# Second FFN of a decay-attention kernel: inner products by pairs of weight tiles and pairs of token blocks, in 11 products in place of 12

## The chip, the cores and the metric

The kernel runs on one core of a Trainium2 chip. Its five engines are TensorE (PE, matrix products), VectorE (DVE), ScalarE (ACT), GpSimd (POOL) and SyncE (SP, which here issues nearly all DMAs). The metric is the device time of one execution in microseconds (us).

## The reference

A linear attention with decay over 4 x 768 tokens of 8 heads x 48, then two FFNs. Only the last one is changed:

```python
def _moe2_ref(x, w_in, w_out):           # x 3072 x 384, w_in 384 x 2048, w_out 2048 x 384
    h = x @ w_in
    sp = np.where(h > 20.0, h, np.log1p(np.exp(np.minimum(h, 20.0))))
    g = h * np.tanh(sp)                  # Mish
    return (g @ w_out).astype(np.float32)
```

## The kernel before

The 3072 tokens are six blocks j of 512 (`NB`), the model width of 384 is three chunks c of 128 (`KC`), and the 2048 hidden columns are 16 tiles f of 128 (`NF2`). Every operand of a large product is held as two fp32r halves, hi (rounded) and lo (the rest), and `product` makes one 128x128x512 product in three matmuls: weight hi by data hi, weight hi by data lo, weight lo by data hi (lines 253 to 255).

The order of the instructions on each engine is the order of the code (`manual_schedule`); buffers are taken from pools, and an instruction waits where its buffer or its data is not free yet. The parts in the order of time are the attention with the first FFN's first units woven in, the first FFN (units of 27 matmuls: `gate`, `val` and `out` of nine each), and the second FFN. While the last 12 units of the first FFN run (block 5), the 32 split weight tiles of the second FFN are read from DRAM (`w2s`) into the pool `wpool`, 36 slots of 384 KB, as the first FFN's weights in it come free, and they stay there for all six blocks.

The second FFN goes over `units2`, all f of block 0, then all f of block 1, and so on. `ffn2_in` makes one inner tile: three products (nine matmuls) summed in one PSUM bank, and one ACT instruction that reads the bank and writes Mish of it to SBUF (line 928). `split_of` makes the halves: hi by ACT (line 934), lo by DVE (line 935). `ffn2_out` adds a tile's three output products (nine matmuls) to three PSUM accumulators `acc0` to `acc2`, three units (`LAG`) later. After a block's last tile the accumulators are copied out, `acc1` by DVE (line 953), the others by ACT (line 955), and stored. The data of the next block comes from DRAM (`load_mid`) and is split chunk by chunk (`split_mid`).

Banks: three in the pool `ps_at` (name `at`), two in `ps_mm` (`mm`), three accumulators (`ps_acc`).

Of the kernel before, what the change touches and what calls it, by code (L numbers as in the profile page):

```python
# [82 lines left out]
def tile_decay_attention_then_two_ffns(  # L83
# [254 lines left out]
    for n in range(B, PRELOAD):  # L338
# [406 lines left out]
    def opens(c):  # L745
# [110 lines left out]
    for n in range(2, len(units) - NF1):  # L856
# [11 lines left out]
        turn = iter(ticks)  # L868
# [8 lines left out]

    LAG = 3  # L880
    hpool = ctx.enter_context(tc.tile_pool(name="hpool", bufs=3))
    g2pool = ctx.enter_context(tc.tile_pool(name="g2pool", bufs=LAG + 2))
    mpool = ctx.enter_context(tc.tile_pool(name="mpool", bufs=KC))

    def load_mid(j):
        raw = []
        for c in range(KC):
            raw.append(mpool.tile([P, NB], F32, name="rows"))
            rows = slice(c * NB, (c + 1) * NB)
            nc.sync.dma_start(out=raw[c], in_=mid[j][:, rows])  # L890
            if j == 1:
                nc.gpsimd.dma_start(out=raw[c], in_=begun[:, rows], accum_op=ALU.add)
        xs[j, "m"] = (
            raw,
            *(xpools[j % 2].tile([P, KC, NB], F32R, name=f"x_{k}") for k in ("hi", "lo")),
        )

    def split_mid(j, c):
        raw, hi, lo = xs[j, "m"]
        nc.vector.tensor_copy(hi[:, c, :], raw[c])  # L900
        nc.vector.tensor_tensor(
            out=lo[:, c, :], in0=raw[c], in1=f32(hi[:, c, :]), op=ALU.subtract
        )

    for f in range(NF1):
        unit1(len(units) - NF1 + f)
        if f == 2:
            load_mid(0)
        if f in (5, 6, 7):
            split_mid(0, f - 5)  # L910
        for n in range(3 if f else 0):
            weights.tick()
    ffn1_out(*units[-1])

    units2 = [(j, f) for j in range(NJ) for f in range(NF2)]
    N2 = len(units2)
    hs, g2 = {}, {}

    def ffn2_in(n):
        j, f = units2[n]  # L920
        _, hi, lo = xs[j, "m"]
        pool, name = ((ps_at, "at"), (ps_mm, "mm"))[n % 5 in (1, 3)]
        ps = pool.tile([P, NB], F32, name=name)
        wt = weights.until((2, f, 0))
        for c in range(KC):
            product(ps, wt, cols(c), hi[:, c, :], lo[:, c, :], c == 0, c == KC - 1)
        h = hs[n] = hpool.tile([P, NB], F32, name="h")
        nc.scalar.activation(h, ps, AF.Mish)  # L928

    def split_of(n):  # L930

        h = hs.pop(n)
        hi, lo = g2[n] = [g2pool.tile([P, NB], F32R, name=f"g_{k}") for k in ("hi", "lo")]
        nc.scalar.activation(hi, h, AF.Copy)  # L934
        nc.vector.tensor_tensor(out=lo, in0=h, in1=f32(hi), op=ALU.subtract)  # L935

    def ffn2_out(n, ms=range(KC)):
        j, f = units2[n]
# [8 lines left out]
    def ffn2_store(n):
        j, f = units2[n]
        if f == NF2 - 1:
            for m in range(KC):  # L950
                o = opool.tile([P, NB], F32, name="o")
                if m == 1:
                    nc.vector.tensor_copy(o, accs[m])
                else:
                    nc.scalar.activation(o, accs[m], AF.Copy)
                nc.sync.dma_start(out=out[j, :, m * NB : (m + 1) * NB], in_=o)

    nc.scalar.preload_act_table_set("mish")
    for n in range(N2 + LAG):
        if n < N2:  # L960
            ffn2_in(n)
        if n == N2 + LAG - 1:

            for m in range(KC):
                ffn2_out(N2 - 2, [m])
                ffn2_out(N2 - 1, [m])
        elif LAG <= n < N2 + LAG - 2:
            ffn2_out(n - LAG)
        if n < N2:
            split_of(n)  # L970
        if n >= LAG:
            ffn2_store(n - LAG)
        j, f = units2[min(n, N2 - 1)]
        if n < N2 and j + 1 < NJ:
            if f == 6:
                load_mid(j + 1)
            if f in (9, 10, 11):
                split_mid(j + 1, f - 9)


# [79 lines left out]
```

## Time and profile before

| what | value |
|---|---|
| median of three runs | 943.07 us (942.3 to 943.15) |
| the profiled execution: time, span of its instructions | 943.3 us, 941.6 us |
| TensorE busy, granted clock | 932.3 us (99%), 1.000 of full speed |
| VectorE, ScalarE, GpSimd busy | 422.1, 334.9, 172.8 us |
| DMA | 94.97 MB, mean 101 GB/s |

Busy time of PE is the union of matmuls that overlap: one lasts 0.39 us from its start to its modelled end, while the next starts long before that end. What a matmul takes of PE's time is the distance between two starts, which a timeline shows. The span is 1.7 us shorter than the execution's own time.

### The profile page before, as it was taken

What the parts mean: (1) busy time and instruction counts of PE and PEld (TensorE: products, weight loads), DVE (VectorE), ACT (ScalarE), POOL (GpSimd) and SP (SyncE); (2) the same over time, 40 slices, a digit from 0 to 9 for tenths busy, and PEclk for the clock granted to TensorE, in tenths of its full rate; (3) what the DMA queues carried; (4) which work ended last, traced back from release to release, by engine and by line L of the source; (5) the groups of instructions that cost most, each with busy time, mean ns of one, the idle gap of its engine ahead of it and who ended that gap; (6) DMA issues with size and microseconds to landing.
All of it is one profiled execution on the core that took longest, in us unless ns stands there. A gap on an engine that the chain in (4) does not pass through costs nothing.

```text
span 941.6 us, 14268 instructions
## 1 busy us (share of the span) xinstructions
PE 932.3 (99%) x5769; PEld 762.0 (81%) x5769; DVE 422.1 (45%) x764; ACT 334.9 (36%) x674; POOL 172.8 (18%) x162
## 2 busy tenths in 40 slices
PE   9999999999999999999999999999999999999998
PEld 6888877778888888888888888888888888888886
DVE  8898978445787777532223222223113212222111
ACT  6765443324343433312221243233332333323322
POOL 4100221665554565420000010000000000000000
PEclk9999999999999999999999999999999999999999
DMA  9454631325674865310066640010010100200000
GB/s 320 145 144 135 227 126 34 136 102 198 197 239 136 273 200 184 136 52 1 1 222 197 185 100 1 1 68 1 0 68 1 63 5 1 68 1 1 34 1 33
DMA packets 36353, 94.97 MB, mean 101 GB/s; under 512 B 4288, under 2 KB 4672, under 8 KB 36288
## 3 DMA queue, kind: packets, MB, share of 16 engines
q1 hardware_dynamic: 35856, 93.28, 30.1%
q0 software_dynamic: 432, 0.79, 0.5%
q8 instruction: 45, 0.74, 0.3%
q14 instruction: 20, 0.16, 0.1%
HBM read 71.24 MB, written 22.81 MB: 100 GB/s over the span
## 4 chain that ended last, share of the span: by engine, by line
PE 97%; DVE 2%; ACT 0%; issue 0%; DMA 0%; DVEq 0%
PE mm L253 13%; PE mm L255 13%; PE mm L254 13%; PE acc L253 12%; PE acc L254 12%; PE acc L255 12%; PE at L253 5%; PE at L255 5%; PE at L254 5%; PE at L537 3%; PE at L488 2%; PE mm L488 1%; PE at L514 1%; PE at L570 1%; PE acc L446 0%; PE at L506 0%
## 5 line engine op out<-in xcount | busy, mean ns | idle before, releaser
L253 PE MATMUL mm<-x_hi,w_split 128*128 128x512 f32 x543 | 214.3, 395 | 0.0
L255 PE MATMUL mm<-x_hi,w_split 128*128 128x512 f32 x543 | 211.6, 390 | 1.3 <-DVE w_split L207 1.3
L254 PE MATMUL mm<-x_lo,w_split 128*128 128x512 f32 x543 | 211.8, 390 | 0.1
L935 DVE TENSOR_TENSOR g_lo<-h,g_hi 128x512 fp32r<-128x512 f32 x96 | 66.4, 692 | 300.2 <-ACT g_hi L934 300.2
L253 PE MATMUL acc<-g_hi,w_split 128*128 128x512 f32 x483 | 189.3, 392 | 0.0
L254 PE MATMUL acc<-g_lo,w_split 128*128 128x512 f32 x483 | 188.3, 390 | 0.3 <-DVE g_lo L689 0.3
L255 PE MATMUL acc<-g_hi,w_split 128*128 128x512 f32 x483 | 188.0, 389 | 0.0
L681 DVE TENSOR_TENSOR o<-mm,o 128x512 f32<-128x512 f32 x72 | 49.6, 689 | 160.9 <-PE mm L255 122.0
L255 PEld LDWEIGHTS mm<-x_hi,w_split 128*128 128x128 f32 x543 | 101.9, 188 | 23.3 <-DVE w_split L207 1.7
L253 PEld LDWEIGHTS mm<-x_hi,w_split 128*128 128x128 f32 x543 | 101.9, 188 | 23.1 <-issue 0.6
L254 PEld LDWEIGHTS mm<-x_lo,w_split 128*128 128x128 f32 x543 | 102.0, 188 | 20.9 <-DVE x_lo L616 0.4
L253 PEld LDWEIGHTS acc<-g_hi,w_split 128*128 128x128 f32 x483 | 90.7, 188 | 19.8 <-ACT g_hi L683 0.2
L254 PEld LDWEIGHTS acc<-g_lo,w_split 128*128 128x128 f32 x483 | 90.7, 188 | 19.6 <-DVE g_lo L689 1.1
L255 PEld LDWEIGHTS acc<-g_hi,w_split 128*128 128x128 f32 x483 | 90.7, 188 | 19.0
L683 ACT ACTIVATE g_hi<-o 128x512 fp32r<-128x512 f32 x72 | 45.5, 633 | 130.3 <-DVE o L681 129.9
L928 ACT ACTIVATE h<-at 128x512 f32<-128x512 f32 x58 | 34.7, 598 | 154.6 <-PE at L255 154.5
L677 ACT ACTIVATE o<-mm 128x512 f32<-128x512 f32 x71 | 42.1, 593 | 97.8 <-PE mm L255 83.4
L254 PE MATMUL at<-x_lo,w_split 128*128 128x512 f32 x174 | 67.7, 389 | 0.0
L253 PE MATMUL at<-x_hi,w_split 128*128 128x512 f32 x174 | 67.7, 389 | 0.0
L255 PE MATMUL at<-x_hi,w_split 128*128 128x512 f32 x174 | 67.7, 389 | 0.0
L689 DVE TENSOR_TENSOR g_lo<-o,g_hi 128x512 fp32r<-128x512 f32 x72 | 54.5, 758 | 23.7 <-ACT g_hi L683 23.7
L934 ACT ACTIVATE g_hi<-h 128x512 fp32r<-128x512 f32 x96 | 60.7, 632 | 3.1
(115 smaller groups left out, 945.9 us busy)
## 6 DMA issues: line engine op xcount, KB each, us to landing
w_raw<-w SPq DMA_DIRECT2D x68, 384.0 KB, 3.6
rkv_sb<-rkv_t SPq DMA_DIRECT2D x16, 768.0 KB, 5.1
w2s<-w_raw SPq DMA_DIRECT2D x32, 384.0 KB, 4.0
w_split<-w2s SPq DMA_DIRECT2D x32, 384.0 KB, 3.5
n_sb<-rk_n SPq DMA_DIRECT2D x16, 384.0 KB, 5.8
mid<-o SPq DMA_DIRECT2D x18, 256.0 KB, 2.2
rows<-mid SPq DMA_DIRECT2D x18, 256.0 KB, 3.6
y<-o SPq DMA_DIRECT2D x18, 256.0 KB, 2.1
```

What stands on the lines that cost most here:

```text
L253: nc.tensor.matmul(acc, lhsT=wt[:, 0, sl], rhs=hi, start=start, stop=False)
L254: nc.tensor.matmul(acc, lhsT=wt[:, 0, sl], rhs=lo, start=False, stop=False)
L255: nc.tensor.matmul(acc, lhsT=wt[:, 1, sl], rhs=hi, start=False, stop=stop)
L488: nc.tensor.matmul(ps[g][:, i, :], lhsT=a["k"][q, i, :], rhs=a["r"][q, i, :], start=True, stop=True,)
L537: nc.tensor.matmul(ps[q * QUAD : (q + 1) * QUAD, c, :], lhsT=lhsT, rhs=rhs, start=q not in begun_q, stop=ends[q] == n, skip_group_check=True,)
L677: nc.scalar.activation(sg, ps, AF.Silu)
L681: nc.vector.tensor_tensor(out=sg, in0=ps, in1=sg, op=ALU.mult)
L683: nc.scalar.activation(hi, sg, AF.Copy)
L689: eng.tensor_tensor(out=lo, in0=sg, in1=f32(hi), op=ALU.subtract)
L928: nc.scalar.activation(h, ps, AF.Mish)
L934: nc.scalar.activation(hi, h, AF.Copy)
L935: nc.vector.tensor_tensor(out=lo, in0=h, in1=f32(hi), op=ALU.subtract)
```

## The change

It takes the tiles f = 2q and 2q+1 and the blocks j = 2p and 2p+1 together: a cell (p, q), three passes p of eight cells. With a(f,c) the weight chunks, b(c,i) the data chunks, the first two of the three chunks are a 2x2 by 2x2 product of 128x128 and 128x512 pieces, which is made by seven products (Strassen's algorithm in Winograd's form) with sums of weights s1 to s4 and differences of data t1 to t4; the third chunk is made by four plain products. That is 11 products or 33 matmuls in a cell, where the same four inner tiles took 12 products or 36 matmuls. The seven results (regions 1, 2, 6, 5, 7, 3, 4 in this order, one bank each) are added up in SBUF tiles: one ACT copy out of PSUM, seven DVE adds; then Mish is taken by ACT in place. These tiles come from `wpool`.

- The sums of weights are made once per q while the last 12 units of the first FFN run (`sums_of`, called by `beside2` after a unit's `out`), split, and stored to DRAM (`w2z`, and s4 over one chunk of `w2s`).
- `wpool` now holds results, and the weights are read again wherever they are used: `Stream` issues a 384 KB load eight loads ahead of its use, three for a cell and one for each output tile, 168 in all.
- The output products keep their order (all f of block 0, then block 1, ...), but their places are given by the list `events`: none in the first cell, two in each other cell of pass 0, four in each cell of passes 1 and 2, and 18 after the last cell. The halves of a result are made up to three output tiles ahead (`LEAD`).
- The data of a pass is loaded in the third cell of the pass before, and its differences and halves are made in the last cell of that pass (`NEXT`) and in its own first cell (`THEN`); those of pass 0 beside the first FFN (`BESIDE2`).

```diff
-    LAG = 3
...
+    NQ = NF2 // 2
+    AHEAD_W, LEAD = 8, 3
...
+    def sums_of(q):
...
+        nc.vector.tensor_tensor(out=n[:, :, 0], in0=n[:, :, 0], in1=n[:, :, 1], op=ALU.add)
...
+            (s1, a21, a22, ALU.add), (s2, s1, a11, ALU.subtract),
+            (s3, a11, a21, ALU.subtract), (s4, a12, s2, ALU.subtract),
+        ):
+            nc.vector.tensor_tensor(out=o, in0=a, in1=b, op=op)
+        if q + 1 < NQ:
+            load_pair(q + 1)
+        nc.scalar.activation(t[:, 0], f32(t[:, 1]), AF.Copy)
+        nc.vector.tensor_tensor(out=t[:, 1], in0=f32(t[:, 1]), in1=f32(t[:, 0]), op=ALU.subtract)
...
+        nc.sync.dma_start(out=to, in_=t[:, :, :3])
+        nc.sync.dma_start(out=src[1][:, :, :P], in_=t[:, :, 3])
...
+            places = {(0, 0): (), (0, 1): (5, 4)}.get((p, min(q, 1)), (2, 5, 3, 4))
+            for r in R_ORDER:
+                events.append(("region", p, q, r))
+                if r in places:
+                    events.append(("out", *outs[n]))
...
+    NEXT = {1: "b11", 2: "b21 b31", 5: "t1 t2", 7: "t3", 3: "b32"}
+    THEN = {1: "b22", 2: "t4 d3"}
...
+    PARTS2 = {
+        1: (("x", 0, "b11"),),
+        2: (("x", 1, "b21"), ("x", 2, "b31")),
+        6: (("z", 1, "t2"),),
+        5: (("z", 0, "t1"),),
+        7: (("z", 2, "t3"), ("y", 2, "b32")),
+        3: (("y", 0, "b22"), ("x", 2, "b32")),
+        4: (("y", 1, "t4"), ("y", 2, "d3")),
+    }
...
+    def region(n, p, q, r):
         pool, name = ((ps_at, "at"), (ps_mm, "mm"))[n % 5 in (1, 3)]
...
+        if r == 1:
+            nc.scalar.activation(g_tile(1, 1), ps, AF.Copy)
+        elif r == 2:
+            more(g_tile(0, 0), us[1, 1], ps)
+            mish(p, q, 0, 0)
+        elif r == 6:
+            more(us[1, 1], us[1, 1], ps)
+        elif r == 5:
+            more(g_tile(0, 1), us[1, 1], ps)
+        elif r == 7:
+            more(g_tile(1, 0), us[1, 1], ps)
+            more(us[1, 1], us[1, 0], us[5])
+            mish(p, q, 1, 1)
...
```

On TensorE, at a step from one inner tile to the next, the program before has (the last product of a tile in bank `at`, the first of the next in bank `mm`):

```order
L253 MATMUL at_5536<-x_hi_5093,w_split_5099 128x512
L254 MATMUL at_5536<-x_lo_5094,w_split_5099 128x512
L255 MATMUL at_5536<-x_hi_5093,w_split_5099 128x512
L253 MATMUL mm_5552<-x_hi_5093,w_split_5139 128x512
L254 MATMUL mm_5552<-x_lo_5094,w_split_5139 128x512
L255 MATMUL mm_5552<-x_hi_5093,w_split_5139 128x512
```

and the changed program begins its first cell with regions 1, 2 and 6 (`x_hi_5438` is b31 here; `w_split_5483` holds the chunks of tile 0, `w_split_5487` the sums s1 to s3):

```order
L250 MATMUL at_5609<-b11_hi_4971,w_split_5483 128x512
L251 MATMUL at_5609<-b11_lo_4972,w_split_5483 128x512
L252 MATMUL at_5609<-b11_hi_4971,w_split_5483 128x512
L250 MATMUL mm_5615<-b21_hi_4973,w_split_5483 128x512
L251 MATMUL mm_5615<-b21_lo_4974,w_split_5483 128x512
L252 MATMUL mm_5615<-b21_hi_4973,w_split_5483 128x512
L250 MATMUL mm_5615<-x_hi_5438,w_split_5483 128x512
L251 MATMUL mm_5615<-x_lo_5439,w_split_5483 128x512
L252 MATMUL mm_5615<-x_hi_5438,w_split_5483 128x512
L250 MATMUL at_5625<-t2_hi_4975,w_split_5487 128x512
L251 MATMUL at_5625<-t2_lo_4976,w_split_5487 128x512
L252 MATMUL at_5625<-t2_hi_4975,w_split_5487 128x512
```

A bank took nine matmuls before and takes three or six now; the matmuls themselves have the same shape.

On VectorE, in one unit of the first FFN's last block, the program before has the product of the gate (681), the lo half (689), and in three of the units a split of the next data:

```order
L681 TENSOR_TENSOR o<-mm,o 128x512
L689 TENSOR_TENSOR g_lo<-o,g_hi 128x512
L900 CAST x_hi<-rows 128x512
L901 TENSOR_TENSOR x_lo<-rows,x_hi 128x512
L681 TENSOR_TENSOR o<-mm,o 128x512
```

and the changed program has, in eight of the 12 units, the sums of weights between the lo half and the next unit's product (678 and 686 are 681 and 689 of before):

```order
L678 TENSOR_TENSOR o<-mm,o 128x512
L686 TENSOR_TENSOR g_lo<-o,g_hi 128x512
L899 TENSOR_TENSOR x_hi<-x_hi 128x2x256
L906 TENSOR_TENSOR x_lo<-x_hi 128x128
L906 TENSOR_TENSOR x_lo<-x_lo,x_hi 128x128
L906 TENSOR_TENSOR x_lo<-x_hi 128x128
L906 TENSOR_TENSOR x_lo<-x_hi,x_lo 128x128
L910 TENSOR_TENSOR x_lo<-x_lo 128x512
L678 TENSOR_TENSOR o<-mm,o 128x512
```

Six instructions have come in ahead of the next product; the last one waits for an ACT copy.

On VectorE at the end of a block in the second FFN, the program before has lo halves alone around the copy of `acc1`:

```order
L935 TENSOR_TENSOR g_lo_5944<-h_5932,g_hi_5943 128x512
L935 TENSOR_TENSOR g_lo_5969<-h_5957,g_hi_5968 128x512
L953 COPY o_5975<-acc1_5565 128x512
L935 TENSOR_TENSOR g_lo_6006<-h_5991,g_hi_6005 128x512
L935 TENSOR_TENSOR g_lo_6031<-h_6019,g_hi_6030 128x512
```

and the changed program reaches the first such copy, in the first cell of pass 1, at the end of a run of 30 instructions that begins with region 2's add in the last cell of pass 0 (its first rows and its last; `rows` are raw data, lines 981 the differences and lo halves, 1059 the adds):

```order
L1059 TENSOR_TENSOR w_split_6260<-w_split_6249,at_6253 128x512
L981 TENSOR_TENSOR b11_lo_4972<-rows_5779,b11_hi_4971 128x512
L1059 TENSOR_TENSOR w_split_6249<-w_split_6249,mm_6266 128x512
L981 TENSOR_TENSOR b21_lo_4974<-rows_5781,b21_hi_4973 128x512
...
L981 TENSOR_TENSOR x_lo_5581<-rows_5783,x_hi_5580 128x512
L1059 TENSOR_TENSOR w_split_6362<-w_split_6362,mm_6402 128x512
L981 TENSOR_TENSOR g_lo_6398<-w_split_5613,g_hi_6397 128x512
L1059 TENSOR_TENSOR w_split_6412<-w_split_6362,at_6408 128x512
L1110 COPY o_6428<-acc1_5715 128x512
```

The copy has moved behind the data work of the next pass and the adds of two cells.

## Rows read from the trace of the kernel before

**Rows 1.** The page's first part: busy us (share of the span) and instructions of engines.

```profile
PE 932.3 (99%) x5769; PEld 762.0 (81%) x5769; DVE 422.1 (45%) x764; ACT 334.9 (36%) x674; POOL 172.8 (18%) x162
```

**Rows 2.** The page's second part: granted TensorE clock in 40 slices.

```profile
PEclk9999999999999999999999999999999999999999
```

**Rows 3.** The page's fourth part: the chain that ended last, by engine.

```profile
PE 97%; DVE 2%; ACT 0%; issue 0%; DMA 0%; DVEq 0%
```

**Rows 4.** Timeline of PE in the second FFN: start us, duration us, instruction.

```profile
545.91 0.39 PE L253 MATMUL at<-x_hi,w_split 128*128 128x512 f32 x1
...
561.78 0.39 PE L254 MATMUL at<-x_lo,w_split 128*128 128x512 f32 x1
562.00 0.39 PE L255 MATMUL at<-x_hi,w_split 128*128 128x512 f32 x1
562.23 0.39 PE L253 MATMUL acc<-g_hi,w_split 128*128 128x512 f32 x1
...
937.36 0.39 PE L255 MATMUL acc<-g_hi,w_split 128*128 128x512 f32 x1
```

**Rows 5.** Groups from 546 us on: count, busy us, mean ns, idle before.

```profile
L253 PE MATMUL at<-x_hi,w_split 128*128 128x512 f32 x174 | 67.7, 389 | 0.0
L935 DVE TENSOR_TENSOR g_lo<-h,g_hi 128x512 fp32r<-128x512 f32 x96 | 66.4, 692 | 300.2 <-ACT g_hi L934 300.2
L934 ACT ACTIVATE g_hi<-h 128x512 fp32r<-128x512 f32 x96 | 60.7, 632 | 3.1
L928 ACT ACTIVATE h<-at 128x512 f32<-128x512 f32 x58 | 34.7, 598 | 154.6 <-PE at L255 154.5 <-issue 0.2
```

**Rows 6.** Groups of the whole span: DVE instructions like the new ones.

```profile
L681 DVE TENSOR_TENSOR o<-mm,o 128x512 f32<-128x512 f32 x72 | 49.6, 689 | 160.9 <-PE mm L255 122.0 <-issue 19.0 <-ACT o L677 15.7
L616 DVE TENSOR_TENSOR x_lo<-at,x_hi 128x384 fp32r<-128x384 f32 x24 | 13.2, 550 | 5.4 <-ACT x_hi L606 4.7 <-ACT x_hi L611 0.6
L586 DVE TENSOR_TENSOR state<-at,state 48x192 f32<-48x192 f32 x32 | 11.3, 352 | 2.5 <-ACT state L593 2.2
```

**Rows 7.** Timeline of DVE in the second FFN, at the end of block 0.

```profile
616.76 0.69 DVE L935 TENSOR_TENSOR g_lo<-h,g_hi 128x512 fp32r<-128x512 f32 x1 [3.39 <-ACT g_hi L934]
617.37 0.68 DVE L953 COPY o<-acc 128x512 f32<-128x512 f32 x1
```

**Rows 8.** Timeline of DVE and ACT in one unit of the first FFN's last block.

```profile
480.61 0.69 DVE L681 TENSOR_TENSOR o<-mm,o 128x512 f32<-128x512 f32 x1 [3.42 <-PE mm L255]
481.34 0.63 ACT L683 ACTIVATE g_hi<-o 128x512 fp32r<-128x512 f32 x1 [2.18 <-DVE o L681]
482.00 0.69 DVE L689 TENSOR_TENSOR g_lo<-o,g_hi 128x512 fp32r<-128x512 f32 x1 [0.70 <-ACT g_hi L683]
486.73 0.69 DVE L681 TENSOR_TENSOR o<-mm,o 128x512 f32<-128x512 f32 x1 [4.04 <-DMA w_split<-w2s]
```

**Rows 9.** DMA from 473 to 546 us: totals; KB each and median us to landing.

```profile
DMA packets 5476, 14.22 MB, mean 195 GB/s; under 512 B 608, under 2 KB 608, under 8 KB 5472
...
w_split<-w2s SPq DMA_DIRECT2D x32, 384.0 KB, 3.5
...
rows<-mid SPq DMA_DIRECT2D x3, 256.0 KB, 4.6
```

**Rows 10.** Timeline where the second FFN begins: DVE, ACT and SP's queue.

```profile
543.21 0.69 DVE L689 TENSOR_TENSOR g_lo<-o,g_hi 128x512 fp32r<-128x512 f32 x1 [0.70 <-ACT g_hi L683]
...
546.73 1.28 ACT L958 ACT_TABLE_LOAD   x1
...
547.10 1.43 SPq L890 DMA_DIRECT2D rows<-mid  x3
```

**Rows 11.** Windows: us, busy and instructions by engine, PE clock, DMA share, GB/s.

```profile
473.00:546.00 73.00, 73.00 (x323) 60.16 (x322) 20.87 (x32) 15.85 (x26) 0.00 (x0) 1.00 0.62 195
```

More of the change, by code (lines that the diff above doesn't have):

```diff
@@ L115, in tile_decay_attention_then_two_ffns @@
     begun = dram.tile([P, KC * NB], F32, name="begun")
+    w2z = [dram.tile([P, 2, DM], F32, name=f"w2z{q}") for q in range(NF2 // 2)]
     ctx.enter_context(tc.manual_schedule())
@@ L875, in tile_decay_attention_then_two_ffns @@
     first.close()
-    LAG = 3
[L881 to L903, printed above, removed]
-    for f in range(NF1):
[L906 to L912, printed above, removed]
-    ffn1_out(*units[-1])
@@ L915, in tile_decay_attention_then_two_ffns @@
[L915 to L921, printed above, removed]
-        pool, name = ((ps_at, "at"), (ps_mm, "mm"))[n % 5 in (1, 3)]
[L923 to L928, printed above, removed]
@@ L930, in split_of @@
-    def split_of(n):
[L932 to L938, printed above, removed]
+    NQ = NF2 // 2
+    AHEAD_W, LEAD = 8, 3
+    tpool = ctx.enter_context(tc.tile_pool(name="tpool", bufs=1))
+    g2pool = ctx.enter_context(tc.tile_pool(name="g2pool", bufs=LEAD + 2))
@@ new lines, in tile_decay_attention_then_two_ffns @@
+    R_ORDER = (1, 2, 6, 5, 7, 3, 4)
+    outs = [(j, f) for j in range(NJ) for f in range(NF2)]
+    events, n = [], 0
+    for p in range(NJ // 2):
+        for q in range(NQ):
+            places = {(0, 0): (), (0, 1): (5, 4)}.get((p, min(q, 1)), (2, 5, 3, 4))
[3 more added lines that the diff above has]
+                    events.append(("out", *outs[n]))
+                    n += 1
+    events += [("out", *o) for o in outs[n:]]
@@ new lines, in tile_decay_attention_then_two_ffns, with __init__, add, ahead @@
+    class Stream:
+        def __init__(self):
+            self.jobs, self.at, self.got, self.place = [], 0, {}, {}
+            for e in events:
+                if e[0] == "out":
+                    self.add(e, w2s[2 * e[2] + 1])
+                elif e[3] == 1:
+                    q = e[2]
+                    for i, src in enumerate((w2s[4 * q], w2s[4 * q + 2], w2z[q])):
+                        self.add(("in", e[1], q, i), src)
+        def add(self, key, src):
+            self.place[key] = len(self.jobs)
+            self.jobs.append((key, src))
+        def ahead(self, n):
+            while self.at < min(n, len(self.jobs)):
+                key, src = self.jobs[self.at]
+                self.got[key] = wpool.tile([P, 2, DM], F32R, name="w_split")
+                nc.sync.dma_start(out=f32(self.got[key]), in_=src)
+                self.at += 1
+        def get(self, key):
+            self.ahead(self.place[key] + 1 + AHEAD_W)
+            return self.got[key]
@@ new lines, in tile_decay_attention_then_two_ffns, with load_mid, place_ops @@
+    stream = Stream()
+    raws, ops = {}, {}
+    def load_mid(p):
+        for i in range(2):
+            j = 2 * p + i
+            for c in range(KC):
+                t = raws[c, i] = mpool.tile([P, NB], F32, name="rows")
+                rows = slice(c * NB, (c + 1) * NB)
+                nc.sync.dma_start(out=t, in_=mid[j][:, rows])
+                if j == 1:
+                    nc.gpsimd.dma_start(out=t, in_=begun[:, rows], accum_op=ALU.add)
+    def place_ops(i):
+        if i < 2:
+            pair = [xpools[i].tile([P, KC, NB], F32R, name=f"x_{k}") for k in ("hi", "lo")]
+            for c, name in enumerate((("b31", "t3", "b32"), ("b22", "t4", "d3"))[i]):
+                ops[name] = [t[:, c, :] for t in pair]
+        else:
+            for name in ("b11", "b21", "t2", "t1"):
+                ops[name] = [tpool.tile([P, NB], F32R, name=f"{name}_{k}") for k in ("hi", "lo")]
@@ new lines, in less, with split, flush, split_mid @@
+    def less(o, a, b):
+        nc.vector.tensor_tensor(out=o, in0=a, in1=b, op=ALU.subtract)
+    late = []
+    def split(pair, src):
+        hi, lo = pair
+        nc.scalar.activation(hi, src, AF.Copy)
+        late.append(lambda: less(lo, src, f32(hi)))
+    def flush(n):
+        for f in late[:n]:
+            f()
+        del late[:n]
+    def split_mid(name):
+        if name == "t1":
+            less(raws[0, 0], raws[0, 1], raws[0, 0])
+            raws["t2"] = mpool.tile([P, NB], F32, name="rows")
+            less(raws["t2"], raws[1, 1], raws[0, 0])
+        elif name == "t3":
+            less(raws[0, 1], raws[1, 1], raws[0, 1])
+        elif name == "t4":
+            less(raws[1, 0], raws[1, 0], raws["t2"])
+        elif name == "d3":
+            less(raws[2, 0], raws[2, 0], raws[2, 1])
+        at = {"b11": (0, 0), "b21": (1, 0), "b31": (2, 0), "t1": (0, 0), "t2": "t2", "t3": (0, 1),
+              "b32": (2, 1), "b22": (1, 1), "t4": (1, 0), "d3": (2, 0)}[name]
+        split(ops[name], raws[at])
@@ new lines, in tile_decay_attention_then_two_ffns, with beside2 @@
+    NEXT = {1: "b11", 2: "b21 b31", 5: "t1 t2", 7: "t3", 3: "b32"}
+    THEN = {1: "b22", 2: "t4 d3"}
+    BESIDE2 = {3: "b11", 5: "b21", NQ + 1: "t1 t2", NQ + 2: "b31 t3", NQ + 3: "b32"}
+    def beside2(f):
+        if 0 < f <= NQ:
+            sums_of(f - 1)
+        if f == NQ:
+            place_ops(0)
+        for name in BESIDE2.get(f, "").split():
+            split_mid(name)
+        flush(len(late))
+        if f > NQ:
+            stream.ahead(3 * (f - NQ))
+    place_ops(2)
+    load_pair(0)
@@ new lines, in tile_decay_attention_then_two_ffns @@
+    load_mid(0)
+    for f in range(NF1):
+        turn = iter((nothing, lambda: beside2(f), nothing))
+        unit1(len(units) - NF1 + f, nothing, lambda: next(turn)())
+    place_ops(1)
+    for name in ("b22", "t4", "d3"):
+        split_mid(name)
+    flush(len(late))
+    ffn1_out(*units[-1])
+    gs2, splits, us = {}, {}, {}
+    PARTS2 = {
[7 more added lines that the diff above has]
+    }
@@ new lines, in g_tile, with more, mish @@
+    def g_tile(f, i):
+        t = us[f, i] = f32(wpool.tile([P, 2, DM], F32R, name="w_split"))
+        us[f, i] = t.rearrange("p w n -> p (w n)")[:, :NB]
+        return us[f, i]
+    def more(o, a, b):
+        nc.vector.tensor_tensor(out=o, in0=a, in1=b, op=ALU.add)
+    def mish(p, q, f, i):
+        t = gs2[2 * p + i, 2 * q + f] = us.pop((f, i))
+        nc.scalar.activation(t, t, AF.Mish)
+    def region(n, p, q, r):
+        pool, name = ((ps_at, "at"), (ps_mm, "mm"))[n % 5 in (1, 3)]
+        ps = us[r] = pool.tile([P, NB], F32, name=name)
+        for k, (w, c, name) in enumerate(PARTS2[r]):
+            wt = stream.get(("in", p, q, "xyz".index(w)))
+            product(ps, wt, cols(c), *ops[name], k == 0, k == len(PARTS2[r]) - 1)
+        if r == 1:
[11 more added lines that the diff above has]
+            mish(p, q, 1, 1)
+        elif r == 3:
+            more(us[0, 1], us[0, 1], ps)
+            mish(p, q, 0, 1)
+        elif r == 4:
+            more(us[1, 0], us[1, 0], ps)
+            mish(p, q, 1, 0)
@@ L939, in ffn2_out @@
+    def split_of(n):
+        g = gs2.pop(outs[n])
+        pool = gpool if n % (LEAD + 4) < 2 else g2pool
+        splits[outs[n]] = [pool.tile([P, NB], F32R, name=f"g_{k}") for k in ("hi", "lo")]
+        split(splits[outs[n]], g)
+    def ffn2_out(j, f, ms=range(KC)):
         if f == 0:
@@ L941, in ffn2_out @@
                 accs[m] = ps_acc.tile([P, NB], F32, name=f"acc{m}")
-        hi, lo = g2[n]
-        wt = weights.until((2, f, 1))
+        hi, lo = splits[j, f]
+        wt = stream.get(("out", j, f))
         for m in ms:
             product(accs[m], wt, cols(m), hi, lo, f == 0, f == NF2 - 1)
[L947 to L956, printed above, removed]
@@ L958, in tile_decay_attention_then_two_ffns, with ffn2_store @@
-    nc.scalar.preload_act_table_set("mish")
[L959 to L978, printed above, removed]
+    def ffn2_store(j):
+        for m in range(KC):
+            o = opool.tile([P, NB], F32, name="o")
+            if m == 1:
+                nc.vector.tensor_copy(o, accs[m])
+            else:
+                nc.scalar.activation(o, accs[m], AF.Copy)
+            nc.sync.dma_start(out=out[j, :, m * NB : (m + 1) * NB], in_=o)
@@ new lines, in tile_decay_attention_then_two_ffns @@
+    nc.scalar.preload_act_table_set("mish")
+    n_out = n_split = n_region = 0
+    for e in events:
+        pending = len(late)
+        fresh = set(gs2)
+        more_ops = ""
+        if e[0] == "region":
+            _, p, q, r = e
+            region(n_region, p, q, r)
+            n_region += 1
+            if p + 1 < NJ // 2:
+                if q == 2 and r == 1:
+                    load_mid(p + 1)
+                if q == NQ - 1:
+                    more_ops = NEXT.get(r, "")
+            if p and q == 0:
+                more_ops = THEN.get(r, "")
+        else:
+            n_out += 1
+            _, j, f = e
+            if n_out < len(outs) - 1:
+                ffn2_out(j, f)
+            elif n_out == len(outs):
+                for m in range(KC):
+                    ffn2_out(j, f - 1, [m])
+                    ffn2_out(j, f, [m])
+            if f == NF2 - 1:
+                ffn2_store(j)
+        while n_split < min(n_out + LEAD, len(outs)) and outs[n_split] in fresh:
+            split_of(n_split)
+            n_split += 1
+        for name in more_ops.split():
+            split_mid(name)
+        flush(pending)
```

21 lines of the change are left out of this document (17 added, 4 removed).

## The prediction

> **What bounds the kernel now.** I read the page's busy shares first: PE is busy for 99% of the span, DVE for 45%, ACT for 36% [rows 1]. A busy share can be full of waiting, so next the clock and the chain of waits: the granted clock stands at its full level, 2.4 GHz, in all 40 slices [rows 2], and 97% of the chain that ended last is PE's own work [rows 3]. What a matmul takes is read from the timeline: starts in the second FFN lie 0.22 or 0.23 us apart, at the step from an inner tile in bank `at` to the output product in `acc0` too, where PE has waits for ACT and DVE to pass [rows 4]. The whole stage says it more exactly. It has 6 x 16 x 18 = 1728 matmuls; the first starts at 545.91, the last at 937.36: 391.45 / 1727 = 0.2267 us each. So this stage is a gapless row of equal matmuls, and its time is their number times 0.2267. The other engines are only there to be in time: 96 lo halves of 0.692 us on DVE, 96 hi halves of 0.632 us and as many Mish of 0.598 us on ACT (58 of them in the row shown) [rows 5].
>
> **What is removed.** Each of the 24 cells has 33 matmuls of the first product in place of 36: 72 matmuls of the same shape. 72 x 0.2267 = 16.3 us. The output products stay as many. The matmuls of the first FFN and of the attention are untouched.
>
> At this place the Trainium skill would give another price. Its page "TensorE: Matmul & The Clock Gate", section "Back-to-back issue gap", gives about 131 ns per matmul of 512 columns for a sustained row of weight loads and matmuls, and 216 ns for matmuls alone. By the 131 ns the gain would be an estimated 9.4 us. The trace has the same instruction 1728 times at 226.7 ns, so the measurement decides.
>
> **What is added, and where it hides.** A cell with four output tiles lasts (33 + 36) x 0.2267 = 15.64 us on PE (16.32 before), a cell of pass 0 with two lasts (33 + 18) x 0.2267 = 11.56 us, and the first cell, with none, 7.48 us.
>
> (a) DVE gets seven adds in a cell, 168 in all. The nearest row is the gate's product, which reads one operand from PSUM and one from SBUF: 0.689 us [rows 6]. With four lo halves that is 11 x 0.69 = 7.6 us of 15.64. Independent DVE instructions follow each other faster than they last: the copy of `acc1` starts 0.61 us after the lo half ahead of it, which lasts 0.69 [rows 7]. I step through DVE's queue with 0.61 and take 0.69 for the bound.
>
> (b) ACT: one copy, four Mish, four hi halves, 5 x 0.598 + 4 x 0.632 = 5.5 us of 15.64 [rows 5]. Hidden.
>
> (c) Banks. Regions go round five banks, so region n waits until region n-5 is read. The bank held longest is region 5's, which the second add of region 7 still reads; its next user is region 2 of the next cell. In a full cell that add ends some 10.4 us after the cell's start, the next user starts at 16.3. Hidden by 5.9 us. In the first cell, without output products, it is close: see (g).
>
> (d) The sums of weights in the first FFN's last block. A unit lasts 27 x 0.2267 = 6.12 us; DVE is free from the end of a lo half (482.69) to the next gate product (486.73), 4.04 us [rows 8]. In there come one add of 512 columns (0.69), four of 128 columns, an ACT copy (0.63) that DVE waits for, and a last subtraction (0.69). The four small ones: not below 0.14 us (a quarter of 0.55 for 384 columns), not above 0.352 (48 x 192) [rows 6]; two are links of a chain, and I take 0.27. Sum: 0.61 + 1.05 + 0.1 + 0.63 + 0.1 + 0.69 = 3.2 us, within 4.04. If it overruns, the gate's product comes late, and PE needs the bank that it frees only when the next `val` begins, 8.16 - 4.99 = 3.2 us after that product ends. But each pair of source loads may only be issued when the four small sums of the pair before are done. A load lands 3.5 us after its issue, the worst row in this stretch is 4.6 [rows 9]; SP takes about 0.48 us to issue one (1.43 for three, [rows 10]). Round: 0.61 + 1.05 + 0.1 + 0.48 + 3.5 = 5.7 us, under the unit's 6.12; with 4.6 it is 6.8, seven rounds slip 5 us, cover is 0.8 + 3.2, and PE would lose about 1 us. I take 0, being nearer to the 3.5 of 384 KB loads (these have 256 KB).
>
> (e) The weights are read again: 168 loads of 393 KB, seven in a cell of 15.64 us (176 GB/s), one in 2.04 us after the last cell (193 GB/s). The row to compare is the last block of the first FFN, where such loads ran at a mean of 195 GB/s for 73 us and landed 3.5 us after issue [rows 9], while PE started 323 matmuls in 73.0 us, the same 0.226 us [rows 11]. So this traffic doesn't slow the matmuls. Each load is issued eight loads ahead; following the slots and SP's queue through the built program, the shortest lead behind the first cells is 71 matmuls, 16.1 us, against 3.5 to 4.6. It is at the store of block 4, where SP waits for the accumulators' copies. Hidden.
>
> (f) The next pass's data: in the last cell of a pass DVE gets seven lo halves and three differences more, in the next cell three and two more. In pass 0 that last cell is 11.56 us long, and DVE has 9 + 10 = 19 instructions: 11.6 us at 0.61, 13.1 at 0.69. DVE falls behind, and the first to need it is PE at `acc1` of block 1's first output tile. From region 2's add (which may start 2.24 us after the last cell's start) the copy of `acc1` is the 30th instruction. Step by step with ACT's waits in it, at a pace of 0.61, it ends at 21.9 us; PE wants it at 11.56 + 10.2 + 0.68 = 22.4 us (the next cell's seven regions but the last, two output tiles, three matmuls). At 0.69 each, 2.24 + 29 x 0.69 + 0.69 = 22.9, with a few of ACT's waits on top up to 23.9: PE would stand for 0.5 to 1.5 us. I take 0.4. At the next change of pass the last cell is 4.08 us longer for two DVE instructions more: 0.
>
> (g) Where the second FFN begins, DVE's last lo half ends at 543.90 [rows 10]. Behind it come seven instructions, and on ACT three halves, two copies and the table load of 1.28 us ahead of region 1's copy, which so ends near 549.5. Five adds and one lo half later region 5's bank is free, at 553.4 (0.61) to 553.9 (0.69). PE wants it after 36 matmuls, 545.91 + 8.16 = 554.07. 0, by a thin margin.
>
> **Sum.** From the profiled execution's own 943.3 us: - 16.3 + 0.4 = 927.4. That execution is 0.2 above the median of 943.07, against which the time is **927.2 us**.
>
> **Rivals.** A difference of 0.2%, 1.9 us, is about what a measurement of this kernel can tell from none.
>
> 1. DVE or ACT is late at the places (d), (f), (g), and PE stands there. For it: margins of 0.2 to 0.6 us, made with a pace from one pair of rows. Against: DVE's load is 49% in a full cell, so it catches up in the next. At the bounds, 1 + 1.5 + 0.5, and as much again where one lateness hands on another: 928.5 to 932, say 929.5.
>
> 2. Slower: the repeated loads become the bound. Before, nothing was loaded in this stage but data. The point from which it decides is seven loads in 16.32 us, 169 GB/s: at 160 GB/s a cell lasts 17.2 us, and 16 full cells and 18 last tiles (2.46 against 2.04) make 943.3 + 16 x 0.9 + 18 x 0.42 = 965. For it: 66 MB in place of 12.6. Against: the 195 GB/s held in [rows 9] was set by how fast slots came free, not by the DMAs.
>
> 3. The change does nothing: each satisfied wait costs PE something. In the built programs 197 matmuls of this stage wait before, 354 after. At 0.1 us each, 157 x 0.1 = 15.7 us would eat the gain: 942.7. Against: the starts in [rows 4] don't widen where waits stand.
>
> 4. A removed matmul is worth less than the mean distance, because the weight load, not the streaming, set the pace of the rest. If it paid 0.13 in place of 0.2267, 943.3 - 9.4 = 934. By the skill's 131 ns named above this is what would come; nothing in the rows bears it out, as PE's starts are even.
>
> **How the numbers follow.** My forecast (PE's row stays gapless but for under 1.5 us) 0.76, rival 1 0.15, rival 2 0.05, rival 3 0.02, rival 4 0.02. The likeliest time is 927.2, its own range 926.3 to 928.5. Low end of the range: no stall at all and the runs' own spread of 0.8 us under the median, 926.0. High end: most of rival 1, 931.0. That leaves out the rest of it and rivals 2 to 4. Faster by over 0.2%: 0.76 + 0.15 + 0.02 = 0.93; within: 0.02; slower: 0.05.
>
> **What would show it.** Right: 1656 matmuls in the second FFN at 0.2267 us; PE waits of under 1.5 us in all from the first FFN's last block on; region adds of 0.69 us; loads landing in 3.5 to 5 us with no PE wait for `w_split`. Wrong: the distance of starts over 0.23 in cells; PE idle behind `acc1`'s copy at the changes of pass, or behind the gate's product in the first FFN's last block; PE waiting for DMA in cells, above all in those with four output tiles; a granted clock under 1.0.

## The result and the profile after

The changed kernel takes **929.77 us** (median of four runs, 928.75 to 930.14) against 942.92 for the kernel before on the same chip (four runs, 942.3 to 943.15): a ratio of 0.986, with 0.9843 to 0.9877 as its 95% interval, 13.2 us less. The profiled execution took 929.78 us with a span of 928.1. The forecast was 927.2, with a range from 926.0 to 931.0.

The page of the changed kernel, answering to [rows 1 to 3]: busy us (share) and instructions of the engines; the granted clock in 40 slices; the chain that ended last.

```profile
PE 917.6 (99%) x5697; PEld 748.1 (81%) x5697; DVE 555.1 (60%) x989; ACT 365.3 (39%) x736; POOL 172.8 (19%) x162
...
PEclk9999999999999999999999999999999999999999
...
PE 92%; DVE 3%; DMA 3%; ACT 1%; issue 1%; SPq 0%; POOL 0%; DVEq 0%; ACTq 0%; POOLq 0%
```

72 matmuls are gone, the clock is at its full level throughout, and DVE has gone from 45% to 60%. The last line is the one to stop at. Before, 97% of the chain was PE's own work; now DVE, DMA and ACT hold 7% of it. Somewhere PE waits for a chain that runs through a transfer.

Where it is, the windows tell: busy time and instructions of the engines, granted clock, DMA share, GB/s. The first stretch is the last block of the first FFN (compare [rows 11]), the others are the cells of the three passes.

```profile
473.00:548.00 75.00, 73.61 (x320) 59.52 (x320) 42.44 (x85) 24.27 (x43) 2.80 (x3) 1.00 0.60 192
548.00:641.00 93.00, 93.00 (x412) 77.00 (x411) 57.08 (x88) 42.98 (x71) 0.00 (x0) 1.00 0.58 204
641.00:766.00 125.00, 125.00 (x553) 103.52 (x552) 68.79 (x109) 50.66 (x89) 0.00 (x0) 1.00 0.59 202
766.00:888.00 122.00, 122.00 (x539) 101.00 (x539) 59.23 (x93) 44.28 (x78) 0.00 (x0) 1.00 0.54 185
```

In the second FFN PE has no idle time at all, beside loads of 185 to 204 GB/s. In the first FFN's last block it started 320 matmuls in 75.0 us, where it started 323 in 73.0 before: 320 x 0.2267 = 72.5, so some 2.5 us were lost. Added up start by start, the distances over 0.2267 make 2.63 us there (0.27 before).

The waits of the two FFN stages from 470 us on: who waited for what, us in total, times, longest.

```profile
ACT x_lo L909 <- DVE x_lo L906: 29.1, 8, 4.5
...
DVE x_lo L906 <- DMA w2s<-x_lo: 6.1, 7, 1.7
...
DVE x_hi L899 <- DMA x_hi<-w2s: 3.0, 6, 0.8
...
PEld mm L250 <- ACT o L674: 2.9, 4, 1.2
...
PE mm L250 <- ACT o L674: 1.3, 2, 0.8
```

Read from the bottom: PE and its weight loads wait for line 674, the Silu that empties a gate's bank; DVE's small sums (L906) wait seven times for the store `w2s<-x_lo`. The timeline links the two: one unit with DVE, ACT, SP's queue and the PE row that waited, and around it the first sums of the first unit (483.74), of the seventh and of the last:

```profile
483.74 0.29 DVE L906 TENSOR_TENSOR x_lo<-x_hi 128x128 f32<-128x128 f32 x1
...
515.92 0.69 DVE L899 TENSOR_TENSOR x_hi<-x_hi 128x512 f32<-128x512 f32 x1 [0.29 <-DMA x_hi<-w2s]
...
518.32 0.29 DVE L906 TENSOR_TENSOR x_lo<-x_hi 128x128 f32<-128x128 f32 x1 [1.71 <-DMA w2s<-x_lo]
...
519.42 0.63 ACT L909 ACTIVATE x_lo<-x_lo 128x512 fp32r<-128x512 f32 x1 [4.52 <-DVE x_lo L906]
...
519.96 0.58 ACT L674 ACTIVATE o<-mm 128x512 f32<-128x512 f32 x1
...
520.09 0.69 DVE L910 TENSOR_TENSOR x_lo<-x_lo 128x512 fp32r<-128x512 f32 x1 [0.75 <-ACT x_lo L909]
...
520.59 0.50 PE L250 MATMUL mm<-x_hi,w_split 128*128 128x512 f32 x1 [0.82 <-ACT o L674]
...
521.42 0.62 SPq L914 DMA_DIRECT2D w2s<-x_lo  x1
...
525.25 0.29 DVE L906 TENSOR_TENSOR x_lo<-x_hi 128x128 f32<-128x128 f32 x1 [1.10 <-DMA w2s<-x_lo]
...
531.72 0.29 DVE L906 TENSOR_TENSOR x_lo<-x_hi 128x128 f32<-128x128 f32 x1 [0.70 <-DMA w2s<-x_lo]
```

The sums are written to the one buffer `t` (`x_lo`), and the next unit's sums may not write it before the store of s4 out of it (L914, the second of two stores) has landed. From the first sum at 518.32 it is 3.10 us to that store's issue (sums, ACT's copy, subtraction, the store ahead of it), and 3.83 more until the next unit's first sum: 6.93 us a round. The first sums of the first and seventh unit start at 483.74 and 525.25, six rounds of 6.92 on average (single ones took 6.43 to 7.76), and a unit lasts 6.12 on PE: the sums fall back by 0.8 us a unit. ACT's queue passes that on: the copy (L909) that waits for the sums stands ahead of the Silu, which starts the moment the copy lets go, without idle time of its own. So PE waits for a bank that an engine 39% busy hasn't read.

The transfers between 473 and 548 us: KB each, median us from issue to landing.

```profile
x_hi<-w2s SPq DMA_DIRECT2D x14, 256.0 KB, 3.2
w2z<-x_lo SPq DMA_DIRECT2D x8, 384.0 KB, 3.6
w_split<-w2s SPq DMA_DIRECT2D x7, 384.0 KB, 6.4
w2s<-x_lo SPq DMA_DIRECT2D x8, 128.0 KB, 3.4
mid<-o SPq DMA_DIRECT2D x3, 256.0 KB, 2.3
```

The loads, whose round the prediction reckoned with, land in 3.2 us. The stores out of `t`, for which it reckoned no round, take about as long, and the last of them is issued 3.1 us after the unit's first small sum, where the loads may go right behind the four small sums.

### The profile page after: what moved, and what is told of

Read it like the earlier page. It is cut to its first block, busy times and chain, and to the rows that moved or that the text cites. A ratio compares the mean times of both kernels' runs of the same rounds, so it can differ in the third digit from the quotient of the medians.

```text
span 928.1 us, 14837 instructions
## 1 busy us (share of the span) xinstructions
PE 917.6 (99%) x5697; PEld 748.1 (81%) x5697; DVE 555.1 (60%) x989; ACT 365.3 (39%) x736; POOL 172.8 (19%) x162
## 4 chain that ended last, share of the span: by engine, by line
PE 92%; DVE 3%; DMA 3%; ACT 1%; issue 1%; SPq 0%; POOL 0%; DVEq 0%; ACTq 0%; POOLq 0%
PE mm L250 12%; PE mm L252 12%; PE mm L251 12%; PE acc L250 11%; PE acc L251 11%; PE acc L252 11%; PE at L251 4%; PE at L252 4%; PE at L250 4%; PE at L534 3%; DMA w2s<-x_lo 3%; PE at L485 2%; PE mm L485 1%; PE at L511 1%; DVE x_lo L906 1%; PE at L567 1%
## 5 line engine op out<-in xcount | busy, mean ns | idle before, releaser
L250 PE MATMUL mm<-x_hi,w_split 128*128 128x512 f32 x497 | 196.8, 396 | 1.4 <-ACT o L674 1.3
L252 PE MATMUL mm<-x_hi,w_split 128*128 128x512 f32 x497 | 193.8, 390 | 1.3 <-DVE w_split L208 1.3
L251 PE MATMUL mm<-x_lo,w_split 128*128 128x512 f32 x497 | 193.9, 390 | 0.1
L1063 ACT ACTIVATE w_split<-w_split 128x512 f32<-128x512 f32 x96 | 60.7, 633 | 173.1 <-DVE w_split L1059 171.0
L1059 DVE TENSOR_TENSOR w_split<-w_split,at 128x512 f32<-128x512 f32 x101 | 69.1, 685 | 79.1 <-PE at L252 76.3
L250 PEld LDWEIGHTS mm<-x_hi,w_split 128*128 128x128 f32 x497 | 93.2, 188 | 24.2 <-ACT o L674 2.9
L252 PEld LDWEIGHTS mm<-x_hi,w_split 128*128 128x128 f32 x497 | 93.3, 188 | 21.5 <-DVE w_split L208 1.7
L251 PEld LDWEIGHTS mm<-x_lo,w_split 128*128 128x128 f32 x497 | 93.3, 188 | 19.0 <-DVE x_lo L613 0.4
L981 DVE TENSOR_TENSOR g_lo<-w_split,g_hi 128x512 fp32r<-128x512 f32 x96 | 65.3, 688 | 30.3 <-ACT g_hi L988 30.3
L1059 DVE TENSOR_TENSOR w_split<-w_split,mm 128x512 f32<-128x512 f32 x67 | 45.9, 685 | 53.6 <-PE mm L252 48.9
L988 ACT ACTIVATE g_hi<-w_split 128x512 fp32r<-128x512 f32 x96 | 57.6, 621 | 10.8 <-PE acc L252 10.2
L168 DVE SCALAR_TENSOR_TENSOR w_num<-w_raw,w_num 128x384 uint32<-128x384 uint32 x68 | 50.9, 749 | 0.0
```

Source lines behind the costliest of these rows:

```text
L168: nc.vector.scalar_tensor_tensor(out=num, in0=raw[:, :, 1], scalar=0x80000000, in1=num, op0=ALU.bitwise_and, op1=ALU.bitwise_or,)
L981: nc.vector.tensor_tensor(out=o, in0=a, in1=b, op=ALU.subtract)
L988: nc.scalar.activation(hi, src, AF.Copy)
L1059: nc.vector.tensor_tensor(out=o, in0=a, in1=b, op=ALU.add)
L1063: nc.scalar.activation(t, t, AF.Mish)
```

## The experiments

The first four kernels ran on one chip beside nine runs of the kernel before (median 943.48 us), the last three on another beside ten (943.24). The ratios are to these medians. The change itself was measured apart from both, so small differences to its 929.77 us are less sure than those within a group.

**One store buffer or one load buffer?** Two kernels undo one suspected wait each. Two buffers for the stores:

```diff
-        t = xpools[0].tile([P, KC, NB], F32R, name="x_lo").rearrange("p c t -> p (c t)")
+        if q % 2:
+            t = tpool.tile([P, 8 * P], F32R, name="t_odd")
+        else:
+            t = xpools[0].tile([P, KC, NB], F32R, name="x_lo").rearrange("p c t -> p (c t)")
```

> The split sums of weights go to one of two buffers by turns, so that a unit's small sums need not wait for the stores of the unit before. Theory A (the round of the store sets the pace of the sums: small sums, ACT copy, subtraction, two issues on SP, a store that lands after 3.4 us, 6.6 us in all against a unit of 6.12): the loss of 2.3 us in the first FFN's last block goes, about 927.4 us. Theory B (the round of the loads: add, small sums, issue, a load that lands after 3.2 us, 5.7 us or more): the pace stays, about 929.7 us.

Two buffers for the loads, issued a unit earlier:

```diff
+        if q % 2:
+            n = f32(tpool.tile([P, 8 * P], F32R, name="n_odd"))
+        else:
...
-        if q + 1 < NQ:
-            load_pair(q + 1)
+        if q + 2 < NQ:
+            load_pair(q + 2)
```

> The source weights of the sums are loaded two units ahead into two buffers by turns; the store buffer stays single. Theory A (the store's round): VectorE still waits for the store in each unit, the time stays near 929.5 us. Theory B (the load's round): the waits for loads and with them PE's waits go, about 927.4 us.

Two store buffers: 927.84 us (927.14 to 928.85, four runs), ratio 0.9834 [0.982, 0.9847]. Two load buffers: 929.7 (929.38 to 930.1, four runs), ratio 0.9853 [0.9839, 0.9866], as the change itself. With two store buffers the second FFN starts at 546.04 in place of 548.69 (0.31 us of that lie ahead of the block), PE lost 0.3 us in the last block in place of 2.63, and the window of the last block is as before the change:

```profile
473.00:546.00 73.00, 73.00 (x322) 60.15 (x321) 43.39 (x86) 24.70 (x44) 2.80 (x3) 1.00 0.62 196
```

With two load buffers no wait for those loads is left in the list; the waits from 470 us on show that the stores still do, and PE with them (L909 is here the small sums):

```profile
DVE x_lo L909 <- DMA w2s<-x_lo: 10.7, 7, 2.5
...
PEld mm L250 <- ACT o L674: 3.4, 4, 1.6
...
PE mm L250 <- ACT o L674: 2.0, 2, 1.1
```

DVE's wait for the store grew from 6.1 to 10.7 us, as it comes to that wait earlier, and PE lost 3.2 us. So the store's round holds, and the load's falls.

**What the sums cost in all.** One kernel leaves the sums out, so that the z weights are plain weights and the output is another; one has both pairs of buffers.

```diff
-                    for i, src in enumerate((w2s[4 * q], w2s[4 * q + 2], w2z[q])):
+                    for i, src in enumerate((w2s[4 * q], w2s[4 * q + 2], w2s[4 * q])):
...
-        if 0 < f <= NQ:
-            sums_of(f - 1)
...
-    load_pair(0)
```

> Leaves out the sums of weights, their loads and their stores; the cells read plain weights in their place, so the output is another. All else is as in the changed kernel. Theories A and B: the first FFN's last block has no PE waits beyond those of the kernel before, about 927.3 us, which is the price of all the rest of the change. Theory C (the loss in this block comes from the loads of data and of the first weights, not from the sums): about 929.5 us.

> Two buffers by turns for the loads and two for the stores of the sums. Theories A and B: about 927.3 us, like the kernel without sums; neither round is left. Theory C: 929.5 us.

Without the sums 926.83 us (926.49 to 927.13, four runs), ratio 0.9822 [0.9809, 0.9835]; with two of both buffers 926.84 (926.49 to 929.76, five runs), ratio 0.983 [0.9815, 0.9845]. PE lost 0.29 and 0.27 us in the last block, as the kernel before did. The sums themselves, six DVE instructions and an ACT copy a unit with their loads and stores, cost nothing that these runs can tell; what costs is the store's round, 929.7 - 926.84 = 2.9 us between the two kernels that differ in the store buffer alone. PE's rows say the same, 3.2 against 0.27 us lost. For the change as it stands, with one buffer of each, the second store buffer gave 929.77 - 927.84 = 1.9 us, and 2.3 us in PE's rows. Why the kernel with two store buffers alone has a median 1.0 us above that with two of both, when PE lost 0.3 us in both, stays open; their runs overlap. The kernel with two of both is the better version: faster than the kernel before by 16.6 us, and than the change by about 2.9, where the two intervals just touch (0.983 [0.9815, 0.9845] against 0.986 [0.9843, 0.9877]).

**Is it ACT's order that brings the lateness to PE?** Here DVE makes the copy, and the single store buffer stays.

```diff
-        nc.scalar.activation(t[:, 0], f32(t[:, 1]), AF.Copy)
+        nc.vector.tensor_copy(t[:, 0], f32(t[:, 1]))
```

> The hi half of the sums of weights is made by VectorE in place of ScalarE, nothing else. If PE's 2.3 us came because the activation of the gate stands behind that copy in ScalarE's order, the wait for it goes and about 927.5 to 928.3 us come, though the sums stay late. If VectorE's own lateness was enough to hold PE, the time stays at 929.8 us.

927.6 us (926.47 to 928.96, four runs), ratio 0.9834 [0.9819, 0.9848]; PE lost 0.30 us in the last block. The timeline of a unit, with the first sums of the first and the last one:

```profile
482.73 0.29 DVE L906 TENSOR_TENSOR x_lo<-x_hi 128x128 f32<-128x128 f32 x1
...
516.25 0.29 DVE L906 TENSOR_TENSOR x_lo<-x_hi 128x128 f32<-128x128 f32 x1 [0.70 <-DMA w2s<-x_lo]
...
517.30 0.43 DVE L909 CAST x_lo<-x_lo 128x512 fp32r<-128x512 f32 x1
...
517.76 0.69 DVE L910 TENSOR_TENSOR x_lo<-x_lo 128x512 fp32r<-128x512 f32 x1
...
520.76 0.60 ACT L674 ACTIVATE o<-mm 128x512 f32<-128x512 f32 x1 [1.03 <-PE mm L252]
...
529.50 0.29 DVE L906 TENSOR_TENSOR x_lo<-x_hi 128x128 f32<-128x128 f32 x1 [0.77 <-DMA w2s<-x_lo]
```

The sums still wait for the store (seven times, 5.1 us in all), but the Silu here waits for PE's gate. The edit does a second thing too: the copy is shorter on DVE, 0.43 against 0.63 us, and DVE waits for no other engine between the sums and the subtraction, so that six rounds take 6.70 us on average in place of 6.92 and less lateness gathers. The kernel of the next experiment separates the two. In this block it is the change as it stands, with the copy on ACT, and in its profiled execution the rounds took 6.73 us:

```profile
483.07 0.29 DVE L906 TENSOR_TENSOR x_lo<-x_hi 128x128 f32<-128x128 f32 x1
...
523.47 0.29 DVE L906 TENSOR_TENSOR x_lo<-x_hi 128x128 f32<-128x128 f32 x1 [1.09 <-DMA w2s<-x_lo]
...
525.11 0.58 ACT L674 ACTIVATE o<-mm 128x512 f32<-128x512 f32 x1
...
525.75 0.50 PE L250 MATMUL mm<-x_hi,w_split 128*128 128x512 f32 x1 [0.44 <-ACT o L674]
```

There PE stood behind the Silu when the sums were 523.47 - 483.07 - 6 x 6.12 = 3.7 us late, and lost 1.75 us in the block. With the copy on DVE they were 529.50 - 482.73 - 7 x 6.12 = 3.9 us late, and PE didn't stand. So at equal lateness it is the copy's place in ACT's queue that brings it to PE.

**Is a matmul worth 0.2267 us in this stage?** Region 1's product is made twice in each of the 24 cells, 72 matmuls more; the first result is overwritten.

```diff
+        if r == 1:
+            wt = stream.get(("in", p, q, 0))
+            product(ps, wt, cols(0), *ops["b11"], True, True)
```

> Region 1 is made twice in each cell, the first result being overwritten by the second: 36 matmuls in a cell again, all else as in the changed kernel. Theory of the forecast (each matmul is worth its distance of 0.2267 us): 72 x 0.2267 = 16.3 us more than the changed kernel, about 946.1 us, so 3 us above the kernel before. Rival (a removed matmul was worth 0.13 us, as the weight load and not the streaming sets the pace): 9.4 us more, about 939.2 us.

946.67 us (944.57 to 947.92, seven runs), ratio 1.0035 [1.0024, 1.0046]: 16.9 us more than the change (by the ratios, each to its own chip's runs of before, 16.5). In the profiled execution the first and the last matmul of the second FFN:

```profile
547.14 0.40 PE L250 MATMUL at<-b_hi,w_split 128*128 128x512 f32 x1
...
938.60 0.39 PE L252 MATMUL acc<-g_hi,w_split 128*128 128x512 f32 x1
```

391.46 us, against 923.82 - 548.69 = 375.13 in the change: 16.33 us for 72 matmuls, 0.2268 each. The removed matmuls were worth what was forecast, and the rest of the change gains nothing by itself: with 36 matmuls it is slower than the kernel before. The profiled execution was the fastest of the seven, so what the others take beyond its 944.57 us isn't in this trace and stays open.

**How much lead do the reloads need?** Two loads ahead in place of eight:

```diff
-    AHEAD_W, LEAD = 8, 3
+    AHEAD_W, LEAD = 2, 3
```

> Weights of the second FFN are loaded two loads ahead of their use, not eight. A cell has seven loads in 15.64 us, so the shortest lead falls from 16 us to about 4 to 5 us. If loads land after 3.5 us as in the kernel before, a few us are lost, 930 to 934 us; if loads in this stage land later, after 5 to 6 us, PE waits in every cell, 940 us or more.

932.18 us (930.77 to 932.64, four runs), ratio 0.9878 [0.9862, 0.9895], 2.4 us more than the change. PE lost 1.22 us in the second FFN, at two places, with this row in the waits and, at the first place, these in the timeline of SP's queue and PE:

```profile
PE acc L250 <- DMA w_split<-w2s: 0.7, 2, 0.5
...
645.63 3.35 SPq L1113 DMA_DIRECT2D y<-o  x3
649.08 0.89 SPq L950 DMA_DIRECT2D w_split<-w2s  x2
...
655.85 0.47 PE L250 MATMUL acc<-g_hi,w_split 128*128 128x512 f32 x1 [0.17 <-DMA w_split<-w2s]
```

The other 1.0 us was lost in the last block (3.63 against 2.63 us), whose stall varied from 1.8 to 3.6 us among the kernels that have it.

The loads landed later than in the change, a median of 5.6 us after their issue against 4.3, which is the case that the expectation priced at 940 us or more. That price didn't come, because the edit does less than its number says. It shortens the lead in the order of the code, but SP doesn't wait for PE's place in that order, only for free buffers and for what it stores. Worked out from the trace, by pairing each load's issue with the first matmul that reads it, the loads were issued a median of 22.9 us ahead of their use (29.1 in the change). Only 4 of the 168 had less than 6 us, the shortest 3.6, and the two at which PE waited stand behind a block's store in SP's queue. So two loads ahead in the order nearly do here; what the kernel loses when every load has a few us alone, no run shows.

## Why the prediction was right, and which step was not

The time lies in the range, but the forecast's own condition, under 1.5 us of PE waits, wasn't met: of the cases that were named it was rival 1 that came, an engine late at place (d), at 929.5 by its reckoning. The likeliest time, 927.2, was missed by 2.6 us, and its own range ended at 928.5; the wide range holds because it took in most of a rival with a chance of 0.15. That this rival's 929.5 lies so near is in part luck: it added up bounds for three places, of which two cost nothing and one more than twice its bound.

- **What is removed**: right. 1656 matmuls from 548.69 to 923.82, 375.13 / 1655 = 0.2267 us each. The 131 ns that the Trainium skill gives in "TensorE: Matmul & The Clock Gate", section "Back-to-back issue gap", hold here neither for the matmuls that stay nor for 72 put back; rival 4 falls.
- **(a), (b)**: right. The groups from 548 us on, answering to [rows 5, 6] (count, busy us, mean ns, idle before): the adds, the lo halves, Mish and the hi halves.

```profile
L1059 DVE TENSOR_TENSOR w_split<-w_split,at 128x512 f32<-128x512 f32 x101 | 69.1, 685 | 79.1 <-PE at L252 76.3 <-DMA w_split<-w2z 1.5
L981 DVE TENSOR_TENSOR g_lo<-w_split,g_hi 128x512 fp32r<-128x512 f32 x96 | 65.3, 688 | 30.3 <-ACT g_hi L988 30.3
L1063 ACT ACTIVATE w_split<-w_split 128x512 f32<-128x512 f32 x96 | 60.7, 633 | 173.1 <-DVE w_split L1059 171.0 <-DMA w_split<-w2s 2.0
L988 ACT ACTIVATE g_hi<-w_split 128x512 fp32r<-128x512 f32 x96 | 57.6, 621 | 10.8 <-PE acc L252 10.2
```

The 168 adds (101 of them in the first row) last 685 ns, predicted 0.69 us. DVE mostly waits for PE and ACT for DVE, as it should be where PE is the bound.
- **(c), (g)**: right. The second FFN in the changed kernel's timeline, its first and last matmul (as in [rows 4]) and the two thin places, here and at (f):

```profile
548.69 0.39 PE L250 MATMUL at<-b_hi,w_split 128*128 128x512 f32 x1
...
555.58 0.69 DVE L1059 TENSOR_TENSOR w_split<-w_split,mm 128x512 f32<-128x512 f32 x1
...
556.85 0.39 PE L250 MATMUL mm<-b_hi,w_split 128*128 128x512 f32 x1
...
646.71 0.69 DVE L1110 COPY o<-acc 128x512 f32<-128x512 f32 x1
...
647.97 0.39 PE L250 MATMUL acc<-g_hi,w_split 128*128 128x512 f32 x1
...
923.82 0.39 PE L252 MATMUL acc<-g_hi,w_split 128*128 128x512 f32 x1
```

Region 7's second add frees region 5's bank at 556.27, 7.58 us after the stage's first matmul; the forecast had 7.5 to 8.0, and PE's use at 8.16. It uses it at 8.16. PE didn't wait.
- **(f)**: the step was right, the value taken from it wrong. The last cell of pass 0 starts at 548.69 + 7.48 + 6 x 11.56 = 625.53 and the next one at 637.09. The copy of `acc1` ends at 647.40, 21.87 us after that (predicted 21.9), and PE's matmul for it starts at 22.44 (22.4). The pace of 0.61 held; the 0.4 us put in for the pace of 0.69 didn't come.
- **(e)**: right. Loads landed a median of 4.3 us (`w2s`) and 3.5 us (`w2z`) after issue in this stage, within 3.5 to 5, at 185 to 204 GB/s; no PE wait for `w_split`, and rival 2 falls. The shortest lead behind the first cells was 15.1 us, right behind the store of block 4 (predicted 16.1, at that place). Rival 3 falls with the same even starts: the satisfied waits cost PE nothing.
- **(d)**: this step failed. Its term was taken as 0, with a bound of about 1 us; PE lost 2.63 - 0.27 = 2.4 us. The round of the loads was reckoned rightly: with two store buffers and one load buffer DVE waits for a load once, for 0.2 us. But the same unit has a second round, that of the stores, which the step left out. By the prediction's own numbers it lasts 1.05 + 0.1 + 0.63 + 0.1 + 0.69 = 2.6 us from the first small sum to the end of the last subtraction, 0.48 for the issue of the first store and 3.5 for the landing of the second: 6.6 us, over the unit's 6.12. That would have shown the round, but not yet a loss: seven rounds slip 3.4 us, within the step's cover of 0.8 + 3.2. Measured, the round was 6.9 us (each of the two issues alone lasted 0.56 to 0.62 us, where 0.48 was reckoned for one) and seven of them slipped 531.72 - 483.74 - 7 x 6.12 = 5.1 us, 1.1 beyond that cover. The rest is the cover itself. It was reckoned for the gate product on DVE; what PE waited for was the Silu on ACT, behind the copy. PE's matmul of 520.59 came 0.98 us late when the sums were 518.32 - 483.74 - 5 x 6.12 = 4.0 us late, so about 3.0 us were covered.

The sum by measured terms: 943.3 - 16.3 + 2.4 = 929.4, against 929.78. The other 0.4 us lie ahead of the change: the last block already starts 0.41 us later than in the profile before, over code that is the same in both. Among the profiled executions of all these kernels that point varies from 467.75 to 468.75 us, 467.75 in one whose code up to there is that of the change (the copy on DVE), so it is put down to the run and not to the change.

## What to carry to other kernels

When work is hidden beside a loop, reckon a round for each buffer that it uses, stores included: from the first write, over the issue and landing of the last transfer that reads it, to the next write; a second store buffer cost SBUF alone here, and was worth 1.9 us with one load buffer and 2.9 with two. Then look in each engine's queue for what stands behind the instruction that waits: an engine that is 39% busy held PE, because a copy for later stood ahead of a read of PSUM that PE needed. A count of matmuls on a gapless PE is the safest term of such a sum, and a margin worked out instruction by instruction at the measured pace came out within 0.1 us.

## What the runs showed of the hardware

- Size alone doesn't tell how long a transfer takes to land in this stretch (473 to 548 us of the changed kernel, medians): stores of 128, 256 and 384 KB took 3.4, 2.3 and 3.6 us, loads of 256 and 384 KB 3.2 and 6.4. The Trainium skill's "SBUF — State Buffer", section "The DMA setup-cost knee", fits a part of about 2 us that doesn't grow with bytes, and 436 GB/s for the rest. Its estimate for the 128 KB store would be 2.3 us; the measured 3.4 decides.
- The small adds of 128x128 last 0.28 to 0.29 us, four tenths of a 128x512 one at a quarter of its size. The Trainium skill's "VectorE: DVE Perf Modes", in its section on the errata of instructions that read SBUF, gives (N + 151) / 0.96 ns for adds of fp32 and names it exact at 512 columns, 691 ns; at 128 it makes an estimated 291. This trace agrees with 685 to 693 and 285 to 292.
- PE's starts stay at 0.2267 us beside 204 GB/s of loads and a DVE that is 61% busy (57.08 of 93 us).
